# Attention and a squared-ReLU MLP on one core: three of four parts of the first weight of blocks 2, 6, 10 and 14 stored with their columns in turn

## The chip, the cores and the metric

The kernel runs on one core of a Trainium2 chip. The metric is the device time of one execution in microseconds (us); the time shown is the median of several runs. The engines are TensorE (PE, whose weight loads are listed apart as PEld), VectorE (DVE), ScalarE (ACT), GpSimd (POOL) and SyncE (SP).

## The reference

Sliding-window attention with a linear distance bias, 8 batches, 8 heads, 576 positions, head size 64, and behind it an MLP on the 4608 tokens of width 512 with an inner width of 2048.

```python
scores = scale * np.matmul(q, k.transpose(0, 1, 3, 2))
mask = (rel >= 0) & (rel < window)                    # window = 128
scores = np.where(mask, scores + bias[None], -1000000000.0)
attn = softmax(scores)                                # max, exp, sum, as usual
x = (attn @ v) as [4608, 512]
h = np.maximum(x @ w_in, 0.0)                         # w_in [512, 2048]
return (h * h @ w_out).astype(np.float32)             # w_out [2048, 512]
```

The two weights come in double precision.

## The kernel before

**Tiling.** The 4608 tokens are cut into 9 chunks of 512, the inner width of 2048 into 16 blocks f of 128. `gemm1(c, f)` (line 194) makes one block of `x @ w_in` for one chunk: 12 matmuls of 128 x 512 into the PSUM tile `g`. `gemm2(c, f)` (line 223) adds one block's share of the output: 12 matmuls into four accumulators `acc`. Each factor is held as two float32r parts, a high and a low one (`wh`, `wl`, `xs[..][:, 0]` and `[:, 1]`, `hh`, `hl`), and three of the four products are summed. So gemm1 runs over four parts `cc` of its weight block (128 rows of `w_in` each), and does `wh` times high, `wh` times low and `wl` times high for each: three matmuls and three weight loads a part.

**The weights in memory.** `weights_load(f)` brings a block of both weights, 512 columns a partition in 8 bytes each, into the tile `raw` by one DMA each. `convert(f)` splits each 8-byte number in place into a low and a high float32r word, five elementwise steps over the whole row on ScalarE, VectorE and, for three blocks, GpSimd. So afterwards the tile `w[f]` is `[128, 2, 512, 2]`: partition, first or second weight, column, low or high word; two neighbouring columns of the same word lie 8 bytes apart. All weights stay in SBUF and are used by all chunks.

**Which columns a matmul gets.** `block(i, f, b)` returns the 128 columns of part b of weight i, low and high. Most parts are a run of 128 columns at 8 bytes. The exception is named by

```python
APART = lambda i, f, b: i == 0 and f % 4 == 0 and b < 2
```

There, in the first weight of blocks 0, 4, 8 and 12, parts 0 and 1 share 256 columns and take them in turn, so that the columns of one part lie 16 bytes apart. `_arrays`, on the host, stores the columns of `w1d` in the order that this view asks for.

**The order of the work.** Before chunk 0's MLP there is a start stage with attention for the first chunks' heads; up to gemm1 of block 15 in chunk 0 the order on all engines is that of a planner with written costs and due times (`start`). After that the order on TensorE is written out in `tile_attn_moe`: for n = 16 and on, gemm1 of the n-th block (counted over all chunks), then gemm2 of block n - 2. Every 8 half steps, behind gemm1 of a block with f % 4 == 3, the attention work of the next head pair is put in: the value products (line 338) and scores (line 392). It lies ahead of the gemm2 of a block with f % 4 == 1, and gemm1 of a block with f % 4 == 0 follows. The last chunk has no more attention to do. The other engines' order is left to the scheduler.

Of the kernel before, what the change touches and what calls it, by code (L numbers as in the profile page):

```python
# [22 lines left out]
NF = DF // 128  # L23
# [15 lines left out]
APART = lambda i, f, b: i == 0 and f % 4 == 0 and b < 2  # L39
# [22 lines left out]
class Kern:  # L62
# [114 lines left out]
    def block(self, i, f, b):  # L177

        w = self.w[f][:, i]
        if APART(i, f, b):  # L180
            w = w.rearrange("p (n j o) t -> p n o j t", n=2, o=2)[:, b // 2, b % 2]
        else:
            w = w[:, 128 * b : 128 * b + 128]
        return w[..., 0], w[..., 1]
# [574 lines left out]
def _consts():  # L759
    r = np.arange(128)  # L760
    own, h = r % 64, (r // 64)[:, None]
    cst = np.zeros((128, CST), np.float32)
    cst[:, 0:128] = np.eye(128)
    keep = own[:, None] >= np.arange(64)[None, :]
    cst[:, 128:192] = np.where(h == 0, keep, ~keep).astype(np.int32).view(np.float32)
    cst[:, 192:256] = NEG
    rel = r[:, None] - r[None, :]
    rel = np.where(rel >= 0, rel, rel + 128)
    for a in range(H):
        cst[:, 256 + 128 * a : 384 + 128 * a] = -rel * (8 * slope(a))  # L770
    later = r[:, None] < r[None, :]
    near = [cst[:, 256 + 128 * a : 384 + 128 * a] for a in range(H)]
    return np.concatenate([cst] + [np.where(late, t, np.float32(NEG)) for t in near for late in (later, ~later)], axis=1)


def _arrays(q, k, v, moe_w_in, moe_w_out):
    a = np.ascontiguousarray
    pairs = lambda x: x.transpose(1, 3, 0, 2).reshape(NP, 128, B * S)
    halo = lambda x: np.concatenate([np.zeros((NP, 128, 128), np.float32), x], axis=2)
    qt, kt = pairs(q), halo(pairs(k))  # L780
    qkd = np.stack([np.concatenate([
        qt[:, :, 512 * c : 512 * c + 256], kt[:, :, 512 * c : 512 * c + 640], qt[:, :, 512 * c + 256 : 512 * c + 512],
    ], axis=2) for c in range(NCH)])
    vt = np.zeros((NP, 1 + B * S // 128, 128, 128), np.float32)
    vt[:, 1:] = v.reshape(B, NP, 2, S, D).transpose(1, 0, 3, 2, 4).reshape(NP, B * S // 128, 128, 128)
    vd = np.stack([vt[:, 4 * c : 4 * c + 5].transpose(0, 2, 1, 3).reshape(NP, 128, 640) for c in range(NCH)])
    w1d = a(moe_w_in.reshape(NCC, 128, NF, 128).transpose(2, 1, 0, 3).reshape(NF, 128, NCC * 128))
    w2d = moe_w_out.reshape(NF, 128, DM).copy()
    for i, w in enumerate((w1d, w2d)):
        for f in range(NF):  # L790
            for n in range(2):
                if APART(i, f, 2 * n):
                    x = w[f, :, 256 * n : 256 * n + 256]
                    x[:] = x.reshape(128, 2, 128).transpose(0, 2, 1).reshape(128, 256).copy()
    return [a(qkd), a(vd), w1d.view(np.int64), w2d.view(np.int64), _consts()]
# [18 lines left out]
```

## Time and profile before

| | before |
|---|---|
| median of 3 runs | 956.03 us (955.96 to 956.26) |
| the profiled execution | 956.69 us, span 955.0 us |
| TensorE busy | 946.8 us, 99% of the span, 6392 matmuls |
| weight loads busy | 796.4 us, 83% |
| VectorE, ScalarE, GpSimd busy | 496.5, 417.6, 214.6 us |
| granted TensorE clock | 1.000 |
| DMA | 95.10 MB, mean 100 GB/s |

How to read it: the span runs from the first to the last instruction of one profiled execution. Weight loads overlap the matmuls, so the two busy times don't add up. A row of a group of instructions names the line, the engine, the operation, the tiles written and read, and the count, then the busy time in us and the mean duration in ns. The ends of matmuls are modelled: what counts for the pace is the distance between their starts, and that is what the chain in order of time shows, whose rows have start, length and count.

### The profile page before, as it was taken

The page shows a single profiled execution, that of the slowest core. Times are in us where ns is not written, and L with a number is a line of the kernel's source. Part 1 is how long each engine was busy: PE and PEld are TensorE (multiplying, and loading weights), DVE is VectorE, ACT ScalarE, POOL GpSimd, SP SyncE. Part 2 cuts the span into 40 slices and gives each one's busy share as a digit, 9 for nine tenths or more (in the row PEclk, how much of TensorE's full clock was granted, in tenths as well). Part 3 has the DMA queues.
Part 4 walks back from the last instruction along what each step waited for, and adds up shares of the span by engine and source line. Part 5 has one row for each costly group of instructions (what it writes and reads, how often), then busy time and mean ns, then how long its engine had stood idle before and what let it go on. Part 6 is the DMA issues. An engine that isn't in the chain of part 4 may idle for free.

```text
span 955.0 us, 17236 instructions
## 1 busy us (share of the span) xinstructions
PE 946.8 (99%) x6392; PEld 796.4 (83%) x6392; DVE 496.5 (52%) x1334; ACT 417.6 (44%) x1107; POOL 214.6 (22%) x254
## 2 busy tenths in 40 slices
PE   9899999999999999999999999999999999999998
PEld 5688888888888888888888888888888888888886
DVE  6998864445545455444544454455545444433222
ACT  7898743333444444434433343334344343332222
POOL 4123331222222222222222222221222212220000
PEclk9999999999999999999999999999999999999999
DMA  9974423322433333222433232333322231111001
GB/s 349 404 274 151 146 67 119 83 64 68 124 84 83 84 88 107 72 77 73 127 84 83 77 108 71 83 83 96 114 74 71 71 95 45 45 45 45 1 1 44
DMA packets 72883, 95.10 MB, mean 100 GB/s; under 512 B 8032, under 2 KB 41952, under 8 KB 72800
## 3 DMA queue, kind: packets, MB, share of 16 engines
q1 hardware_dynamic: 72368, 93.36, 32.9%
q8 instruction: 50, 0.82, 0.4%
q10 hardware_dynamic: 432, 0.66, 0.2%
q14 instruction: 33, 0.27, 0.1%
HBM read 67.76 MB, written 26.21 MB: 98 GB/s over the span
## 4 chain that ended last, share of the span: by engine, by line
PE 95%; DMA 4%; ACT 0%; issue 0%; DVE 0%; SPq 0%; DVEq 0%
PE acc L223 42%; PE g L194 42%; PE at L338 6%; PE s L392 3%; PE g L392 2%; DMA raw<-in_dram 2%; DMA wide<-in_dram 1%; DMA qk<-in_dram 1%; PE at L392 0%; ACT raw L165 0%; DVE raw L167 0%; ACT t L426 0%; ACT t L419 0%; ACT o L229 0%; DVE xu L304 0%
## 5 line engine op out<-in xcount | busy, mean ns | idle before, releaser
L194 PE MATMUL g<-xu,w 128*128 128x512 f32 x1728 | 423.3, 394 | 0.8 <-issue 0.8
L194 PEld LDWEIGHTS g<-xu,w 128*128 128x128 f32 x1728 | 344.1, 209 | 56.2 <-issue 1.5
L223 PE MATMUL acc<-hh,w 128*128 128x512 f32 x1152 | 386.2, 396 | 0.0
L223 PEld LDWEIGHTS acc<-hh,w 128*128 128x128 f32 x1152 | 223.9, 194 | 44.3 <-issue 0.7
L207 DVE TENSOR_TENSOR r<-r 128x512 f32<-128x512 f32 x129 | 103.0, 799 | 248.2 <-ACT r L204 246.9
L204 ACT ACTIVATE r<-g 128x512 f32<-128x512 f32 x144 | 85.9, 596 | 326.8 <-PE g L194 316.4
L223 PE MATMUL acc<-hl,w 128*128 128x512 f32 x576 | 226.8, 394 | 0.0
L326 POOL TENSOR_SCALAR_AFFINE_SELECT pp<-pp 128x512 f32<-128x512 f32 x128 | 107.1, 840 | 211.1 <-DMA pp<-way 162.2
L213 DVE TENSOR_TENSOR hl<-r,hh 128x512 fp32r<-128x512 f32 x144 | 108.6, 754 | 69.3 <-ACT hh L211 68.4
L262 POOL TENSOR_TENSOR t<-t,nm 128x512 f32<-128x512 f32 x64 | 82.0, 1281 | 263.9 <-DVE nm L259 145.9
L223 PEld LDWEIGHTS acc<-hl,w 128*128 128x128 f32 x576 | 112.0, 194 | 19.9
L251 ACT ACTIVATE t<-t,nm 128x128 f32<-128x128 f32 x256 | 100.1, 393 | 56.8 <-DVE nm L244 56.8
L211 ACT CAST hh<-r 128x512 fp32r<-128x512 f32 x144 | 89.1, 619 | 75.8 <-DVE r L207 74.2
L438 DVE COPY_PREDICATED t<-cst,s 64x256 f32<-64x256 int32 x100 | 44.5, 445 | 41.0 <-ACT t L426 22.4
L313 DVE STREAM_TRANSPOSE pp<-t 128x512 f32<-128x512 f32 x64 | 45.2, 707 | 38.0 <-POOL t L262 37.9
L338 PEld LDWEIGHTS at<-pp,v 128*64 128x64 f32 x1024 | 55.2, 137 | 11.2 <-issue 10.8
L338 PE MATMUL at<-pp,v 128*64 128x128 f32 x1024 | 63.0, 276 | 0.0
L244 DVE CUSTOM_DVE_ANT_0 t<-t,cst 128x128 f32<-128x128 f32 x256 | 59.0, 293 | 1.0
L251 ACT ACTIVATION_READ_ACCUMULATOR t<-t,nm 128x1 f32 x256 | 48.3, 189 | 0.0
L392 PE MATMUL s<-qk 64*64 64x64 f32 (+2 forms) x1168 | 47.5, 251 | 0.8 <-ACT raw L165 0.8
L392 PEld LDWEIGHTS s<-qk 64*64 64x64 f32 x1168 | 43.0, 133 | 1.0 <-ACT raw L165 1.0
L428 POOL MEMSET t<- 64x128 f32 (+1 forms) x44 | 10.0, 228 | 138.7 <-PE g L392 129.8
(63 smaller groups left out, 472.6 us busy)
## 6 DMA issues: line engine op xcount, KB each, us to landing
raw<-in_dram SPq DMA_DIRECT2D x32, 512.0 KB, 8.7
way<-pp SPq DMA_DIRECT2D x256, 64.0 KB, 1.8
pp<-way SPq DMA_DIRECT2D x64, 256.0 KB, 2.8
qk<-in_dram SPq DMA_DIRECT2D x32, 320.0 KB, 3.6
v<-in_dram SPq DMA_DIRECT2D x32, 320.0 KB, 3.0
qk<-in_dram SPq DMA_DIRECT2D x38, 256.0 KB, 4.2
out_dram<-o SPq DMA_DIRECT2D x35, 256.0 KB, 4.3
v<-in_dram SPq DMA_DIRECT2D x3, 256.0 KB, 4.9
```

The costliest lines, as they stand in the source:

```text
L194: nc.tensor.matmul(g, w, xs[cc][:, part], start=i == 0, stop=i == 11)
L204: self.relu = nc.scalar.activation(r, g, AF.Relu)
L207: nc.vector.tensor_tensor(r, r, r, op=ALU.mult)
L211: nc.scalar.copy(hh, r)
L213: nc.vector.tensor_tensor(hl, r, hh.bitcast(F32), op=ALU.subtract)
L223: nc.tensor.matmul(self.acc[m], w, h, start=(f == 0 and i == 0), stop=(f == NF - 1 and i == 2))
L244: self.nc.vector.tensor_tensor_reduce(self.t[:, m], self.t[:, m], self.K.nrel(2 * self.p + m // 2), -0.125, BIG, ALU.add, ALU.min, self.nm ...
L251: return self.nc.scalar.activation(self.t[:, m], self.t[:, m], AF.Exp, bias=nm[:, m : m + 1], scale=-1.0, accum_out=nm[:, 4 + m : 5 + m],)
L262: self.nc.gpsimd.tensor_tensor(self.t, self.t, self.nm[:, 8:12].unsqueeze(2).to_broadcast([128, 4, 128]), op=ALU.mult)
L326: nc.gpsimd.affine_select(to, self.own, pattern=[[-32 * sign, 4], [0, 4], [-sign, 32]], compare_op=op, fill=0.0, base=0, channel_multiplie ...
L338: self.nc.tensor.matmul(self.X[r, o : o + 128].rearrange("p (a c) -> p a c", a=4), v[:, 2 * sg + k, r], src[:, :, 2 * j + i], start=sg == ...
L392: mm = nc.tensor.matmul(to, qk[r, q0 : q0 + 64], qk[r, k0 : k0 + 64 * n], start=True, stop=True, skip_group_check=True,)
```

## The change

In blocks 2, 6, 10 and 14 the first three parts of the first weight share 384 columns and take them in turn: column j of part b is at place 3j + b, so the columns of one part lie 24 bytes apart in place of 8. Part 3 of these blocks stays a run at 8 bytes. The host stores the columns in that order.

```diff
     def block(self, i, f, b):
 
         w = self.w[f][:, i]
-        if APART(i, f, b):
+        if i == 0 and f % 4 == 2 and b < 3:
+            w = w[:, 0:384].rearrange("p (j o) t -> p o j t", o=3)[:, b]
+        elif APART(i, f, b):
             w = w.rearrange("p (n j o) t -> p n o j t", n=2, o=2)[:, b // 2, b % 2]
         else:
             w = w[:, 128 * b : 128 * b + 128]
...
     w1d = a(moe_w_in.reshape(NCC, 128, NF, 128).transpose(2, 1, 0, 3).reshape(NF, 128, NCC * 128))
+    for f in range(2, NF, 4):
+        x = w1d[f, :, 0:384]
+        x[:] = x.reshape(128, 3, 128).transpose(0, 2, 1).reshape(128, 384).copy()
     w2d = moe_w_out.reshape(NF, 128, DM).copy()
```

## The prediction

> **What bounds the kernel now.** I read the page first: span, busy shares, granted clock, the chain that ended last, the costliest groups.
>
> ```profile
> span 955.0 us, 17236 instructions
> PE 946.8 (99%) x6392; PEld 796.4 (83%) x6392; DVE 496.5 (52%) x1334; ACT 417.6 (44%) x1107; POOL 214.6 (22%) x254
> PEclk9999999999999999999999999999999999999999
> PE 95%; DMA 4%; ACT 0%; issue 0%; DVE 0%; SPq 0%; DVEq 0%
> L194 PE MATMUL g<-xu,w 128*128 128x512 f32 x1728 | 423.3, 394 | 0.8 <-issue 0.8
> L194 PEld LDWEIGHTS g<-xu,w 128*128 128x128 f32 x1728 | 344.1, 209 | 56.2 <-issue 1.5
> L223 PEld LDWEIGHTS acc<-hh,w 128*128 128x128 f32 x1152 | 223.9, 194 | 44.3 <-issue 0.7
> ```
>
> TensorE is 95% of the chain and all of it after the start, at full clock. What counts is the interval from one matmul to the next. The mean load tells more: 209 ns at L194 and 194 at L223, for the same tile shape. L194 already has columns 16 bytes apart in blocks 0, 4, 8 and 12. So I asked for line 194 in two windows of the last chunk, first the start of block 4 (spaced), then that of block 5 (not).
>
> ```profile
> L194 PEld LDWEIGHTS g<-xu,w x7: 194/309/311, 879.0 to 880.4; 128*128 128x128 f32 x7
> L194 PEld LDWEIGHTS g<-xu,w x6: 194/194/194, 884.5 to 885.7; 128*128 128x128 f32 x6
> ```
>
> The numbers are minimum, median and maximum. A load at 16 bytes is recorded with 309 ns, one at 8 bytes with 194. What that does to the matmuls stands in the chain in order of time (start, length, twelve matmuls a row; g is gemm1, acc is gemm2). Undisturbed, in the last chunk:
>
> ```profile
> 871.08 2.76 PE acc L223 x12
> 873.84 2.76 PE g L194 x12
> 876.60 2.76 PE acc L223 x12
> 879.36 2.79 PE g L194 x12
> 882.15 2.76 PE acc L223 x12
> ...
> 901.48 2.79 PE g L194 x12
> 904.27 2.76 PE acc L223 x12
> ...
> 923.59 2.79 PE g L194 x12
> ```
>
> 2.76 us for twelve is 230 ns each. The group with six loads at 16 bytes takes 0.03 more. Finer: from 879.36 to 923.59 lie 16 groups, 44.23 us, two of them spaced; 16 x 2.76 is 44.16, so a spaced group costs 0.035 us, 5.8 ns for each of its six loads. So although a load's record grows by 115 ns, the matmul interval grows by 6: the record of one load overlaps the next, and its pace still nearly fits under the 230 ns of a matmul.
>
> A second thing shows around the attention stages in mid-kernel and in the first chunk.
>
> ```profile
> 212.94 3.02 PE acc L223 x12
> 215.96 2.79 PE g L194 x12
> 218.76 2.76 PE acc L223 x12
> 221.52 2.76 PE g L194 x12
> 224.28 2.76 PE acc L223 x12
> 227.04 2.76 PE g L194 x12
> 229.80 2.76 PE acc L223 x12
> 232.56 2.75 PE g L194 x12
> 235.31 1.90 PE at L338 x32
> ```
>
> ```profile
> 49.86 2.80 PE acc L223 x12
> 52.66 2.80 PE g L194 x12
> 55.46 2.80 PE acc L223 x12
> 58.27 2.79 PE g L194 x12
> 61.06 2.76 PE acc L223 x12
> 70.70 3.02 PE g L194 x12
> 73.72 2.80 PE acc L223 x12
> 99.07 2.80 PE g L194 x12
> 101.87 2.80 PE acc L223 x12
> 111.76 3.14 PE g L194 x12
> 125.40 2.80 PE g L194 x12
> 128.20 2.80 PE acc L223 x12
> 131.00 2.80 PE g L194 x12
> ```
>
> There are two beats: 2.80 per group (233 ns) after a break in the stream, and 2.76 (230 ns) from a spaced group on (58.27 is block 4 of chunk 0; 215.96 is block 12 of chunk 1). The loose beat goes on by itself, 49.86 to 58.27, until a spaced group ends it. Block 12 of chunk 0, at 111.76, is spaced and comes right after a break: 3.14 where the unspaced group after a break, 70.70, has 3.02. There the first load lies open, and its 0.12 more is the 115 ns of the record.
>
> **The change part by part.** Instructions, waits, DMAs and their sizes stay: the host stores three parts of w1 in another order inside the same row, the convert steps work element by element over the whole row, and the view given to the matmul has a step of 24 bytes in place of 8. Cost of all that: nothing; no queue is passed by anything.
>
> What changes is 9 loads in a group (three parts of three matmuls), in 4 groups of each of 9 chunks: 324 loads of the 3456 at lines 194 and 223.
>
> *Price of a load at 24 bytes.* No row shows it. From below: 194 ns, the 8-byte row, and no cost. From above: growth in proportion to the distance, 115 ns more for another 8 bytes, 424 ns. The 309 ns load runs at a pace of 230 + 6 = 236, so some 73 ns of its record lie beside the next; 424 - 73 is 351, which is 121 over a matmul. Nine of them are 1.09 us, 36 groups 39 us. I take the nearest row, the 16-byte one, 309 ns and 5.8 ns in the interval: from 4-byte-wide columns at 8 to 16 bytes the load slows because neighbours no longer come together, and at 24 they are no more apart in that sense than at 16. That is my reading, not a row.
>
> The Trainium skill, SBUF — State Buffer, section Specifications (TRN2), says the same in its own terms: lines of 16 bytes, at least two hits on a line for full bandwidth, a penalty for each crossing; by it 16 and 24 bytes both have one hit a line and the sum is the one below, where growth with distance gives +39 us. The trace agrees for 8 against 16 (194 against 309); no run here shows 24.
>
> *Chunks 1 to 8.* The changed groups (blocks 2, 6, 10, 14) start in the tight beat already: 227.04 is block 14 of chunk 1, with 2.76 before and behind it. So there is no loose beat left to end, and the cost is bare: 9 x 5.8 = 0.052 us a group, 32 groups, +1.66 us. Nothing hides it, since every group is on the chain; a 2.76 group becomes 2.81.
>
> *Chunk 0.* Here they meet the loose beat. Block 2 (the group ahead of 49.86) and block 6 (70.70) come right after a break, so their first load lies open: +0.12 each, from 3.14 against 3.02. Blocks 10 and 14 (99.07, 125.40) run at 2.80 and would stay there within 0.02. If each ends in the tight beat, the groups up to the next break or spaced group save 0.04: three behind block 2 (49.86, 52.66, 55.46), one behind block 6 (73.72), three behind block 10 (101.87 and the two after it), two behind block 14 (128.20, 131.00); nine, -0.36. Sum -0.36 + 0.24 + 0.02 = -0.10, between +0.26 (no beat is changed) and -0.36.
>
> *Sum.* +1.66 - 0.10 = +1.56 us on the profiled execution, whose own time is 956.69 (span 955.0 and 1.7 around it): 958.25. That execution lies 0.66 above the median of the runs, 956.03, so against the median 957.6, or +0.16%. No change can be told from noise within 0.2%, here 1.91 us.
>
> **The rivals.**
>
> *The load costs nothing (no change at all).* The interval rose by only 6 ns for 115 ns more load, so a load a little cheaper than the 16-byte one would fit under the matmul whole. Against it: at 24 bytes no neighbours come nearer than at 16. Time: 956.0, less up to 0.36 if the beat in chunk 0 tightens all the same, so 955.7 to 956.0. The Trainium skill, TensorE: Matmul & The Clock Gate, section LDWEIGHTS, gives a load's time as columns by 1.2 GHz, 107 ns, with no term for spacing, which would also be this case; the trace differs (194 and 309 for the same 128 columns).
>
> *The load becomes the bound (slower).* Place: the nine matmuls of each changed group. It decides as soon as the pace of a load at 24 bytes passes about 237 ns: (1.91 + 0.10) us over 32 groups is 63 ns a group, 7.0 a load against 5.8 measured at 16. At half the growth with distance the loss is 20 us (976), at the full 39 us (995). For it: the 16-byte load is already over the matmul by 6 ns, so all that it adds is paid. Against: no row shows growth with distance beyond the step from 194 to 309.
>
> *The group ends in the loose beat (slower).* Ending a spaced stretch tight is what the chain shows for blocks 0, 4, 8, 12 in the stream; with nine loads in place of six, at another spacing, the hand-over could fall otherwise. For it: the loose beat persists once entered. Price: two groups to the next break (229.80, 232.56) at 2.80 and the last three matmuls, 0.09 us, in 28 groups, 2.5 us; the last chunk has no breaks, so three groups to the next spaced one, and five at its end, 0.6 us. With 1.66 and +0.26 in chunk 0: +5.0, 961.0.
>
> *A third, tighter beat (faster).* 16 bytes took 2.80 to 2.76; a different load could shorten it again. It would need another 0.04 in each of the two or three groups that follow, 36 x 0.10 = -3.6, with the price +1.6: 954.0. Against it: 2.76 is the floor in all rows of the last chunk, whatever came before.
>
> **How the numbers follow.** Forecast as the 16-byte price: 0.62, centre 957.6, from 957.0 (price 5, full gain in chunk 0) to 958.5 (price 7, no gain there); about a quarter of it lies over 957.94, so 0.46 within 0.2% and 0.16 slower. No cost: 0.09, within. Loose beat: 0.10, slower. Load-bound: 0.15, slower. Tighter beat: 0.04, faster. That is 0.04 faster, 0.55 same, 0.41 slower. The range 955.7 to 961.2 holds the first three, 0.81; the two left out are 0.19. The likeliest case alone is 957.0 to 958.5.
>
> **What would show it.** Loads of line 194 at the start of blocks 2, 6, 10, 14: a median near 309 proves the price, 194 the no-cost rival, over 350 the load-bound one. In the chain, the row at 227.04 should read 2.81 with 2.76 behind it; 2.80 behind it is the loose beat, 3 or more is the load bound. In chunk 0 the rows 101.87 and 128.20 should drop to 2.76 and 70.70 rise to about 3.14. The L194 load mean should rise from 209 to about 209 + 115 x 324 / 1728 = 231, the counts of matmuls, loads and DMA packets stay. The prediction is wrong if a load at 24 bytes is not the load at 16: everything else is small beside it.

## The result: 962.09 us, slower by 0.63%

| | before | after |
|---|---|---|
| median of 6 runs | 956.05 us (955.96 to 956.26) | 962.09 us (961.86 to 962.28) |
| ratio, 95% interval | | 1.0063 (1.0052 to 1.0073) |
| the profiled execution | 956.69 us, span 955.0 | 962.28 us, span 960.6 |

The page of the changed kernel (lines 194 and 223 are now 196 and 225):

```profile
span 960.6 us, 17232 instructions
PEclk9999999999999999999999999999999999999999
L196 PE MATMUL g<-xu,w 128*128 128x512 f32 x1728 | 427.0, 396 | 0.8 <-issue 0.8
L196 PEld LDWEIGHTS g<-xu,w 128*128 128x128 f32 x1728 | 359.1, 230 | 45.0 <-issue 1.5
```

The loads, the DMA packets and the clock are as before; the four instructions fewer are matmul records of line 121, in the start stage, of which this trace has 28 and the one before 32. The mean load at L196 went from 209 to 230 ns (231 was forecast). Line 196 over the nine changed loads of block 2 of chunk 4 (minimum, median, maximum):

```profile
L196 PEld LDWEIGHTS g<-xu,w x9: 303/306/312, 460.1 to 462.0; 128*128 128x128 f32 x9
```

So a load at 24 bytes is recorded with 306 ns, like one at 16 (309). The chain in order of time, around block 14 of chunk 1 (start, length, twelve matmuls a row):

```profile
219.98 2.76 PE acc L225 x12
222.74 2.76 PE g L196 x12
225.50 2.77 PE acc L225 x12
228.27 2.82 PE g L196 x12
231.09 2.80 PE acc L225 x12
233.89 2.80 PE g L196 x12
236.69 1.90 PE at L340 x32
```

The group at 228.27 is the changed one: 2.82 for 2.76, and 0.005 in the row ahead, where its first load falls. What the forecast did not put there are the 2.80 in the two groups behind it, up to the break at line 340. Before, both ran at 2.76 (229.80 and 232.56). The last chunk, without breaks, shows it with no other cause near:

```profile
873.10 2.82 PE g L196 x12
875.92 2.80 PE acc L225 x12
878.72 2.80 PE g L196 x12
881.52 2.80 PE acc L225 x12
884.32 2.79 PE g L196 x12
887.12 2.76 PE acc L225 x12
```

Three groups at the loose beat, until the 16-byte loads of block 4 (884.32) end it. In chunk 0 blocks 10 (99.77) and 14 (126.13) start loose and stay loose, and block 6 (71.27), right behind a break, pays for its open first load:

```profile
99.77 2.83 PE g L196 x12
102.60 2.80 PE acc L225 x12
...
126.13 2.83 PE g L196 x12
128.96 2.80 PE acc L225 x12
```

```profile
71.27 3.14 PE g L196 x12
74.41 2.81 PE acc L225 x12
```

**Where the 5.6 us of the span are**, from the starts of the loads in both traces, summed by kind of group: the 32 changed groups of chunks 1 to 8 +2.05 (0.064 each); gemm2 of blocks 0 mod 4 behind them +1.23 and gemm1 of blocks 3 mod 4 +1.54; the groups of chunk 0 +0.36; the start stage before the first gemm1 +0.44 (its first load at 37.66 for 37.22; the other kernels of this study have 37.03 to 37.74, so this can't be told from spread). Together 5.6. The work in the breaks is the same to 0.03 us.

### The profile page after: what moved, and what is told of

Its sections match the earlier page's. It is cut to its first block, busy times and chain, and to the rows that moved or that the text cites. A ratio compares the mean times of both kernels' runs of the same rounds, so it can differ in the third digit from the quotient of the medians.

```text
span 960.6 us, 17232 instructions
## 1 busy us (share of the span) xinstructions
PE 952.0 (99%) x6388; PEld 812.9 (85%) x6392; DVE 498.8 (52%) x1334; ACT 417.6 (43%) x1107; POOL 214.7 (22%) x254
## 4 chain that ended last, share of the span: by engine, by line
PE 95%; DMA 4%; ACT 0%; issue 0%; DVE 0%; SPq 0%; DVEq 0%
PE acc L225 42%; PE g L196 42%; PE at L340 6%; PE s L394 3%; PE g L394 2%; DMA raw<-in_dram 2%; DMA wide<-in_dram 1%; DMA qk<-in_dram 1%; PE at L394 0%; ACT raw L165 0%; ACT t L428 0%; PE acc L293 0%; ACT t L421 0%; ACT o L231 0%; DVE xu L306 0%
## 5 line engine op out<-in xcount | busy, mean ns | idle before, releaser
L196 PE MATMUL g<-xu,w 128*128 128x512 f32 x1728 | 427.0, 396 | 0.8 <-issue 0.8
L196 PEld LDWEIGHTS g<-xu,w 128*128 128x128 f32 x1728 | 359.1, 230 | 45.0 <-issue 1.5
```

What stands on the lines that cost most here:

```text
L196: nc.tensor.matmul(g, w, xs[cc][:, part], start=i == 0, stop=i == 11)
```

## Experiments

Each of three sets of four kernels ran with its own runs of the kernel before; differences are medians of one set. "Loose" and "tight" are the beats of 2.80 and 2.76 us a group; a "stretch" is a run of spaced loads without a plain one between them, and a "break" a stage of attention work in the stream. What a group costs is read from the starts of its twelve loads; each load starts about one interval ahead of its matmul, so the chain's rows differ from it by some ns. The diffs of runs 3, 5 to 8 and 11 are against the changed kernel, the others against the kernel before. The rows shown are those of block 2 of chunk 4 and of what follows, unless said otherwise.

### 1. Six loads at 16 bytes: pairs16

```diff
-APART = lambda i, f, b: i == 0 and f % 4 == 0 and b < 2
+APART = lambda i, f, b: i == 0 and f % 4 in (0, 2) and b < 2
```

> Blocks 2, 6, 10 and 14 get the form that blocks 0, 4, 8 and 12 have: two parts in turn, 16 bytes apart, six spaced loads in place of the change's nine at 24. Theory A (the spacing of 24 bytes is what leaves the loose beat behind): the groups of blocks 2 mod 4 take 2.79 and the two groups behind them 2.76; 32 x 0.035 = +1.1 us, with chunk 0 about 957.2. Theory B (the count of nine loads): the same, 957.2. Theory C (a spaced group that is entered from the tight beat in mid-stream ends loose, whatever its form): 2.80 in the two groups behind, 28 x 0.09 + 0.6 more, about 960.4.

957.87 against 956.65: +1.22 us, ratio 1.0013 (1.0003 to 1.0022).

```profile
458.87 2.79 PE g L194 x12
461.66 2.76 PE acc L223 x12
464.42 2.75 PE g L194 x12
```

Tight behind, in all 32 groups. Theory C falls: a stretch entered tight in mid-stream need not end loose. The price of six 16-byte loads is 0.033 us, for 0.035 in the forecast.

### 2. Nine loads at 16 bytes: nine16

```diff
-APART = lambda i, f, b: i == 0 and f % 4 == 0 and b < 2
+APART = lambda i, f, b: i == 0 and (f % 4 == 0 and b < 2 or f % 4 == 2 and b < 3)
```

> In blocks 2 mod 4 three parts are read at 16 bytes, nine spaced loads as in the change, at the other spacing. (The fourth part is read as a plain run that holds other columns, so its product is left wrong; loads and matmuls are the same in number and shape.) Theory A (spacing): the group takes 2.81, the groups behind it 2.76, about 957.7. Theory B (count): the groups behind run at 2.80, 961 to 962 as with the change.

959.11 against 956.65: +2.46 us, ratio 1.0025 (1.0015 to 1.0035).

```profile
459.06 2.81 PE g L194 x12
461.86 2.76 PE acc L223 x12
```

Tight behind: theory B, the count, falls. A group costs 0.051 us, the forecast's 0.052. The time is 0.8 over the expectation. In the trace, the break behind the stretch starts 0.009 later than with six spaced loads (28 x 0.009 = 0.25 us), and in the last chunk the six-load stretches of blocks 4, 8 and 12 end loose, 0.14 us each:

```profile
878.66 2.76 PE acc L223 x12
881.42 2.81 PE g L194 x12
884.23 2.80 PE acc L223 x12
```

That is block 4 of the last chunk, with no break near. It has the same six loads at 16 bytes as in the kernel before, it is entered from the tight beat, and it ends loose, where before it ended tight (879.36). So six loads at 16 bytes don't always hand back the tight beat.

### 3. Six loads at 24 bytes, places 0 and 1: six24

```diff
-        if i == 0 and f % 4 == 2 and b < 3:
+        if i == 0 and f % 4 == 2 and b < 2:
```

> In blocks 2 mod 4 two parts are read at 24 bytes and the third as a plain run (which holds other columns, so the product of that part is left wrong): six spaced loads, at 24 bytes. Theory A (spacing): the groups behind run at 2.80; the group itself 2.80 (62 ns x 6/9 = 41 ns over 2.76); about 960.7. Theory B (count): six loads end in the tight beat, 2.76 behind, about 957.4.

958.33 against 956.65: +1.68 us, ratio 1.0017 (1.0007 to 1.0026).

```profile
458.82 2.79 PE g L196 x12
461.62 2.76 PE acc L225 x12
```

Tight behind, in all 32 groups of chunks 1 to 8: theory A in its plain form falls too. The 24 bytes alone don't leave the loose beat.

### 4. No spaced group: none

```diff
-APART = lambda i, f, b: i == 0 and f % 4 == 0 and b < 2
+APART = lambda i, f, b: False
```

> No group is spaced: blocks 0, 4, 8 and 12 too are read at 8 bytes. The theory that the loose beat goes on until a spaced group ends it: every group behind a break is at 2.80 up to the next break, six groups of 0.04 in 28 stretches (+7.0 us), the last chunk loose throughout (34 x 0.04, less the four spaced groups' 0.14: +1.2), chunk 0 about +0.2; 964.4. If the loose beat ended by itself, the time would fall by the price of the spaced groups, 36 x 0.035 = 1.2 us, to 954.8.

962.23 against 956.65: +5.6 us, ratio 1.0058 (1.0043 to 1.0073).

```profile
448.80 2.76 PE g L194 x12
...
474.38 2.80 PE g L194 x12
477.18 2.80 PE acc L223 x12
```

The loose beat goes on by itself, as expected; but behind 8 of the 29 breaks from the end of chunk 0 on (448.80 follows one) the stream came out tight without help, so the loss is 5.6 and not 8.4. The loose beat thus costs far more here than the 36 spaced groups of the kernel before, whose own price is 36 x 0.035 = 1.2 us.

### 5. The places in the order 0, 2, 1: order021

```diff
-            w = w[:, 0:384].rearrange("p (j o) t -> p o j t", o=3)[:, b]
+            w = w[:, 0:384].rearrange("p (j o) t -> p o j t", o=3)[:, [0, 2, 1][b]]
...
```

> The changed kernel with the three places of the 384 columns read in the order 0, 2, 1 (place = first column of the part, 0, 8 or 16 bytes into the row); the host stores them to match, the result is the same. Nine loads at 24 bytes as before, but the stretch ends at place 1, as in the run with six loads that ended tight. Theory D (the place of the last spaced part decides the beat behind it): 2.76 behind the group; about 0.065 x 32 = +2.1 us on the kernel before. Theory E (nine loads at 24 bytes end loose, wherever the last one begins): 2.80 behind, +6.0 as the change.

961.82 against 956.22: +5.6 us, ratio 1.0059 (1.0044 to 1.0074).

```profile
459.71 2.83 PE g L196 x12
462.54 2.80 PE acc L225 x12
```

Loose, though it ends at place 1. Theory D falls. The group itself costs 0.077 us in place of 0.064. In chunk 0, blocks 10 and 14 are entered from the loose beat, and there the same nine loads end tight, where those of the change stayed loose (99.77, 126.13):

```profile
99.12 2.82 PE g L196 x12
101.95 2.76 PE acc L225 x12
```

So theory E is no rule either: the beat that a stretch is entered from has a part in the beat that it leaves.

### 6. The order 2, 1, 0: order210

```diff
-            w = w[:, 0:384].rearrange("p (j o) t -> p o j t", o=3)[:, b]
+            w = w[:, 0:384].rearrange("p (j o) t -> p o j t", o=3)[:, [2, 1, 0][b]]
...
```

> The changed kernel with the places read in the order 2, 1, 0, so that the stretch ends at place 0; the result is the same. Theory D: the beat behind need not be that of the change; if places 0 and 2 differ, 2.76 and about +2.1 us, if only the position modulo 16 bytes counts, 2.80 and +6.0. Theory E: 2.80, +6.0.

963.03 against 956.22: +6.8 us, ratio 1.0071 (1.0055 to 1.0086).

```profile
460.30 2.84 PE g L196 x12
463.14 2.81 PE acc L225 x12
```

Loose, and dearer: 0.086 us a group. The same nine loads make a group cost 0.064, 0.077 or 0.086 us by their order alone. Most of that difference lies behind them: the nine intervals themselves are 65, 67 and 72 ns over 9 x 230, and the three that follow in the group -1, 11 and 15.

### 7. Six loads at 24 bytes, places 1 and 2: six24_12

```diff
-        if i == 0 and f % 4 == 2 and b < 3:
-            w = w[:, 0:384].rearrange("p (j o) t -> p o j t", o=3)[:, b]
+        if i == 0 and f % 4 == 2 and b < 2:
+            w = w[:, 0:384].rearrange("p (j o) t -> p o j t", o=3)[:, b + 1]
```

> Two parts at 24 bytes, read at places 1 and 2 in place of 0 and 1; the third is a plain run (the parts get one another's columns, so these products are left wrong; loads and matmuls are the same in number and shape). Six loads, ending at place 2 as the change does. Theory D: 2.80 behind the group, 40 ns x 32 + 3.1 = +4.4 us. Theory E: six loads end tight, +1.7 as with places 0 and 1.

962.17 against 956.22: +6.0 us, ratio 1.0061 (1.0046 to 1.0076).

```profile
460.55 2.82 PE g L196 x12
463.36 2.80 PE acc L225 x12
```

Loose with six loads: theory E falls as well. Count and spacing are those of run 3; only the starts of the columns differ, by 8 bytes. The six intervals cost 51 ns in place of 38.

### 8. A 16-byte stretch behind the changed group: repair

```diff
-APART = lambda i, f, b: i == 0 and f % 4 == 0 and b < 2
+APART = lambda i, f, b: f % 4 == 0 and b < 2
```

> The changed kernel, and in the second weight of blocks 0, 4, 8 and 12 two parts in turn at 16 bytes: a spaced stretch in the gemm2 group that follows each changed group. If the loose beat behind the changed group lasts only until the next spaced stretch, that gemm2 group takes 2.79 and the gemm1 group behind it 2.76 in place of 2.80: 28 x 0.05 + 0.4 = 1.8 us back, +4.2 us on the kernel before. If the loose beat comes back by itself, nothing is won and the six loads cost 1.2 more, +7.2.

963.11 against 956.22: +6.9 us, ratio 1.0071 (1.0054 to 1.0088).

```profile
460.75 2.82 PE g L196 x12
463.57 2.83 PE acc L225 x12
466.40 2.81 PE g L196 x12
```

The stretch at 463.57 has the form that ends the loose beat in blocks 0 mod 4, and here it doesn't. So a spaced stretch is no switch, and the single intervals have to be read.

**The intervals.** From the starts of the matmul records, in ns, from the interval in which the first spaced load runs; the bar stands where the stretch ends. The group is block 2 of chunk 4 (in repair the gemm2 group behind it) unless said otherwise.

```
16 bytes
pairs16, 6     231 235 241 231 235 241 | 231 229 231 229            tight
nine16, 9      231 235 241 231 235 241 230 235 241 | 231 229 231    tight
before, 6      236 236 235 234 235 241 | 231 229 231 229            tight
 (block 4 of chunk 1, entered loose)
nine16, 6      232 234 235 241 231 235 | 238 233 233 234            loose
 (block 4 of the last chunk)
repair, 6      238 235 234 235 241 231 | 235 234 240 233 242 235 230 236 234 233 233   loose
24 bytes
six24, 6       235 239 244 231 235 235 | 232 229 231 229            tight
six24_12, 6    237 243 237 241 239 234 | 235 232 227 232 233 234    loose
after, 9       235 238 244 231 235 235 238 240 239 | 231 231 227 232 234   loose
order210, 9    237 240 238 237 238 242 236 235 239 | 230 235 240 233 242 235 230   loose
```

At 16 bytes a stretch settles into a cycle of 235, 241, 231. The tight ends have 241 before the bar. The loose end of run 2 has 235 there: its cycle lies one interval behind that of run 1. Repair enters one step further in the cycle than the kernel before, ends behind 231, and then runs through the series 235 234 240 233 242 235 230 that also follows many breaks, into the loose beat. From that came theory G and a forecast: entered as in run 1, five and seven loads must end loose where six and nine end tight.

### 9. Five loads at 16 bytes: five16

```diff
             for w, part in ((wh, 0), (wh, 1), (wl, 0)):
+                if f % 4 == 2:
+                    v = self.w[f][:, 0]
+                    far = v.rearrange("p (n j o) t -> p n o j t", n=2, o=2)[:, cc // 2, cc % 2]
+                    w = (far if i < 5 else v[:, 128 * cc : 128 * cc + 128])[..., 0 if i % 3 == 2 else 1]
```

> Blocks 2 mod 4: only the first five loads are at 16 bytes, the sixth (the low words of the second part) and all others are plain runs (the plain ones hold other columns in part, so the products are left wrong; loads and matmuls are the same in number and shape). Theory G (the beat behind a stretch depends on where in the spaced loads' own cycle of intervals, 235, 241, 231 ns, the stretch ends: tight behind 241, as with six and nine loads): five loads end on 235, so 2.80 behind; 0.03 x 32 + 3.1 = +4.0 us on the kernel before. Theory S (a stretch at 16 bytes entered from the tight beat ends tight, whatever its length): 2.76 behind, +0.9.

961.40 against 956.07: +5.3 us, ratio 1.0056 (1.0041 to 1.0071).

```profile
459.61 2.81 PE g L198 x12
462.42 2.80 PE acc L227 x12
```

Loose in all 32: one spaced load fewer than in run 1 costs 4.1 us more (each against its own runs of before). Theory G holds, S falls.

### 10. Seven loads at 16 bytes: seven16

The same with `i < 7`.

> The same with the first seven loads at 16 bytes (the first of the third part with them; products left wrong as there). Theory G: the stretch ends on 231, 2.80 behind, 0.04 x 32 + 3.1 = +4.4 us. Theory S: +1.3.

962.29 against 956.07: +6.2 us, ratio 1.0065 (1.0050 to 1.0080).

```profile
460.60 2.83 PE g L198 x12
463.43 2.80 PE acc L227 x12
```

Loose in all 32, by the series 235 234 240 233 242 235 230, as in repair. Both sums came out 1 to 2 us low. In the traces the loose tail inside the group, which I had not counted, is 0.9 us with five loads and 1.1 with seven, and chunk 0 costs another 0.3; the rest is not placed.

Over all traces together, the 16-byte stretches that don't begin right behind a break fit theory G without an exception: 506 end on an interval of 239 to 242 ns, and all are tight behind; 42 end on 234 to 236 and 66 on 229 to 232, and all are loose. Of 34 that begin right behind a break, 9 don't fit: block 0 of chunk 0 before, for one, ends on 234 and is tight.

### 11. Eight loads at 24 bytes: eight24

```diff
             for w, part in ((wh, 0), (wh, 1), (wl, 0)):
+                if f % 4 == 2 and i == 8:
+                    w = self.w[f][:, 0, 256:384, 0]
```

> The changed kernel with one load less at 24 bytes: the ninth, the low words of the third part, is a plain run (it holds other columns, so that product is left wrong). Theory G: the end falls one step earlier in the cycle, on the 240 ns interval in place of 238, 231; if a late interval is what ends tight, 2.76 behind and about 0.06 x 32 = +2 us. Theory S (24 bytes with place 2 in it ends loose): 2.80 behind, about +5.5.

962.45 against 956.07: +6.4 us, ratio 1.0067 (1.0050 to 1.0084).

```profile
460.63 2.83 PE g L198 x12
463.46 2.80 PE acc L227 x12
```

Loose: the intervals are 235 238 244 231 235 235 239 240 | 238 233 234 233. A late interval ahead of the bar isn't enough at 24 bytes. This run's theory S got its 2.80, but blocks 10 and 14 of chunk 0 in run 5 have place 2 and end tight. Theory G told the end of 16-byte stretches; for 24 bytes I have no rule.

### 12. Twelve loads at 32 bytes: twelve32

```diff
-        if APART(i, f, b):
+        if i == 0 and f % 4 == 2:
+            w = w.rearrange("p (j o) t -> p o j t", o=4)[:, b]
+        elif APART(i, f, b):
...
```

> Blocks 2 mod 4 with all four parts in turn, 32 bytes apart, twelve spaced loads; the result is the same. If a load's price grows with the distance beyond 16 bytes: a record of some 540 ns at L196 and matmul intervals over 400 ns, +70 us or more. If every distance of 16 bytes and more costs the same: records near 309 ns, 6 to 10 ns an interval, 12 x 36 of them, +2.6 to +4.3 us, and 3.1 more if the group ends loose.

965.96 against 956.07: +9.9 us, ratio 1.0104 (1.0089 to 1.0119). Line 196 over the twelve loads, and the chain:

```profile
L196 PEld LDWEIGHTS g<-xu,w x12: 317/328/336, 461.7 to 464.4; 128*128 128x128 f32 x12
462.08 2.94 PE g L196 x12
465.02 2.80 PE acc L225 x12
```

The record is 328 ns for 309 at 16 bytes: no growth in proportion to the distance, but some. The group costs 0.164 us, 13.7 ns a load, over twice the 16-byte price, and ends loose.

## Why the prediction was wrong

**The step that failed** is the one under chunks 1 to 8, that the cost there is bare: I let every changed group hand back the tight beat in which it began. It does not; two groups behind each run loose, +2.8 us in the trace. This was the third rival, named with the right place (the two groups up to the break, three in the last chunk) and given 0.10. My ground for the bare cost was that the spaced stretches in the stream end tight. But these were one kind of stretch, the same six loads at 16 bytes; 31 of the 36 were entered from the loose beat and only three, in the last chunk, from the tight one, as the changed groups are. So they are far fewer than 36 cases, and run 2 has the same six loads entered tight and ending loose. The stretch at block 12 of chunk 0 (111.76), right behind a break, could have warned me: the next six intervals of its group are 238, 233, 233, 234, 233, 233 ns, the loose beat. What makes nine loads at 24 bytes hand over loose stays open: spacing, count and last place alone each fell as the reason.

**The size of a load.** 5.8 ns were taken, 7.1 measured in the order of the change (0.064 / 9): 2.05 us for 1.66. That term lies inside the bounds given, and the mechanism, a 16-byte record and a small excess in the interval, was right: 306 ns for 309. The load-bound rival and the no-cost rival both fall. The rival's own sum, 961.0, had the 5.8 in it; with 7.1 it would have been 961.4.

**Chunk 0.** -0.10 was taken, +0.36 measured. The open first load was right (71.27: 3.14), but none of the four stretches ended tight, so nothing came back; +0.26 was the bound for that, 0.1 short.

**The rest.** Nothing else moved: counts, clock, breaks. The forecast of +1.6 us against +6.0 measured is thus 2.8 us of loose beat, 0.4 of load price, 0.5 of chunk 0, and 0.4 in the start stage that can't be told from spread. The remaining 0.4 lies between the two traces and the medians: the profiled execution before lies 0.6 over its median, the one after 0.2.

By the rule of the Trainium skill on lines of 16 bytes (SBUF — State Buffer, section Specifications (TRN2)), loads at 16, 24 and 32 bytes all have one hit a line, so the same price. The records at 16 and 24 bytes agree (309 and 306 ns), the intervals nearly (5.6 ns over 230 in run 2, 7.1 in the change); at 32 bytes, 328 ns and 13.7 ns, they differ. The Trainium skill, TensorE: Matmul & The Clock Gate, section LDWEIGHTS, makes a load's time depend on the columns alone. That does not hold here: 194, 309, 306 and 328 ns for the same 128 columns at 8, 16, 24 and 32 bytes.

## What to carry to other kernels

When TensorE bounds a kernel, read the distance between matmul starts before and behind every irregular stretch, since a stretch can cost more in the groups behind it than in itself. A rhythm that one pattern is seen to bring about is evidence for that pattern with its entry and its length, and not for the like of it; one load more or less decided here between +1.2 and +5.3 us. A layout that is cheaper load by load need not be the faster one: this kernel without any spaced load was 5.6 us slower. So time a layout by the groups that follow.

## What the runs showed of the hardware that I had not expected

- The stream of 128 x 512 float32r matmuls has two beats, 230.0 and 233.3 ns, at the same clock and with the same loads (194 and 196 ns); in the kernel without spaced loads each holds up to the next break. There the stream stays loose behind 21 of 29 breaks and is tight behind 8.
- What a spaced stretch at 16 bytes leaves behind goes with the place in its cycle of intervals where it ends, and so with its length to the single load and with its entry: in blocks 2 mod 4 of chunks 1 to 8, 6 and 9 loads end tight and 5 and 7 loose, in all 32 groups of each run; with the cycle one interval behind, 6 end loose (run 2, 3 groups). Right behind a break it can fall otherwise. Why the hand-over falls so, no run here shows.
- A group with the same nine loads at 24 bytes costs 64, 77 or 86 ns by the order of their starts in the row, 65, 67 or 72 of it in the nine intervals. Entered from the loose beat, the order 0, 2, 1 ends tight (2 of 2 groups); entered from the tight one, loose (32 of 32). That is left open too.
